# Attention scores in a fused attention and MLP kernel: one 64-row matmul per head, two heads in turn into two PSUM banks

## The chip, the cores and the metric

The kernel runs on one core of a Trainium2 chip. The metric is device time in microseconds (us) of one execution; before the change it is 1000.22 us, the median of three runs.

## The reference

```
k_p = k.reshape(B, H, Sp, 8, D).mean(axis=3)      # B = 8 batches, H = 8 heads, S = 576 tokens, D = 64
v_p = v.reshape(B, H, Sp, 8, D).mean(axis=3)      # Sp = 72 pooled keys
scores = scale * np.matmul(q, k_p.transpose(0, 1, 3, 2))
attn = np.exp(scores - max); attn = attn / (sum + 1e-09)
x = (attn @ v_p), heads side by side              # 4608 tokens x 512
h = x @ w_in                                      # 512 x 2048
out = (h * sigmoid(1.702 * h)) @ w_out            # 2048 x 512
```

All inputs are float32 or, for the weights, float64 on the way in; the output is 4608 x 512 float32.

## The kernel before

Two parts share the core. The first is attention; it writes `x`, transposed, as pairs of float32r values (a high and a low part). The second is the MLP: `moe_in` (L555 to L573) multiplies 128 columns of `w_in` by chunks of 256 or 384 tokens into PSUM tiles `h`, and `moe_out` (L575 to L589) multiplies by `w_out` into PSUM tiles `o`. Each MLP product is three float32r passes (L563 to L565, L583 to L585). The MLP loop at the end of the kernel goes over the steps of all chunks, and after each step it calls `pump()` some five times; a pump runs the attention generator up to its next `yield`. A chunk of the MLP cannot start before its tokens of `x` are written, and attention may not run further ahead than two buffers of `x`. The framework then orders the instructions of each engine with a timeline of its own, so that code order is a priority rather than an order.

Attention goes batch by batch, and each batch in two pieces of tokens: piece 0 has two tiles of 128 tokens, piece 1 two tiles of 128 and one of 64. In the code `j` counts the four pairs of heads. For a pair, `turned_q(j)` makes `qt`, the queries turned to 128 rows (64 columns of head 2j, then 64 of head 2j+1) by tokens; from the second batch on this is a DVE transpose (L296) of a tile `qr` that four DMAs fetch. `sum_keys` and `turn_keys` make `m.k2`, in which each pair has 128 rows by 144 columns on a block diagonal: rows 0 to 63 hold the first head's keys in columns 0 to 71, rows 64 to 127 the second head's in columns 72 to 143, and zeros stand elsewhere. So `score` (L305) needs one matmul per pair and tile of tokens: the stationary operand is `qt` (128 rows by 128 or 64 tokens), the moving one `m.k2[:, j]`, and the 144 columns of the result are both heads' scores. Scores are plain float32 matmuls. `less_most` (L317) then takes each head's maximum on DVE (L320) and subtracts it on the way from PSUM to the SBUF tile `sc` (L321); ACT's exponential (L354), sums and the normalised `main` and `tail` follow (L359, L381, L389).

`qt` and `qr` have two buffers each. The PSUM pool `ps_a` has three banks, which the scores (`sps`), the turned keys (`kps`) and the weighted values (`pav`, L452 to L455) share. Between the pairs the generator yields, so `score(j)`, `turned_q(j + 2)` and `less_most` of pair j take turns with MLP work.

Of the kernel before, what the change touches and what calls it, by code (L numbers as in the profile page):

```python
# [22 lines left out]
def attention_moe_kernel(ctx: ExitStack, tc: tile.TileContext, q, k, v, w_in, w_out, out):  # L23
    """Every float32 product is three float32r passes: an operand x is hi + lo, hi the rounding of
    x to 12 significant bits and lo the exact rest, and hi*hi + hi*lo + lo*hi carries float32's bits."""
# [15 lines left out]
    # Tokens of a batch in two pieces, and each piece's tiles of tokens: first token and count.  # L41
# [6 lines left out]
    OVER = 192  # tokens of a piece beyond its first chunk, at most  # L48
# [7 lines left out]
    # The chunks of tokens of the second part: first token and count.  # L56
# [63 lines left out]
    def fetch_q(b, piece, j, place=None):  # L120
        """Quadrants of 32 partitions: a head of the pair and half of its columns each."""
# [14 lines left out]
    def spread(b, raw, bd, nm):  # L136
        """The window sums of 64 keys of each head, each pair's two heads on a block diagonal."""
# [31 lines left out]
    def fetch_first():  # L169
        """The first batch, where x and the last parts of the weights will lie; q as it is."""  # L170
# [93 lines left out]
    written = [0]  # tokens whose x is complete  # L264
    unstaged = []

    def attention(b, piece, whole_q=None):
        """In stages; each yield says which chunk must be through before the next stage, or how far it is."""
# [36 lines left out]
        def score(j, qt):  # L305
            ps = ps_a.tile([P, 512], F32, tag="a", name=f"sps{n}_{j}")
            for t, (s0, ns) in enumerate(tiles):
                nc.tensor.matmul(  # L308
                    ps[:ns, t * PW : (t + 1) * PW],
                    lhsT=qt[:, s0 - o0 : s0 - o0 + ns],  # L310
                    rhs=m.k2[:, j],
                    start=True,
                    stop=True,
                )
            return ps

        def less_most(hs, views):  # L317
            for (ns, g), pv in zip(groups, views):
                nt, nh = g.stop - g.start, hs.stop - hs.start
# [4 lines left out]
                    in1=nm[:ns, g, hs].unsqueeze(3).broadcast_to([ns, nt, nh, KEYS]),  # L324
# [7 lines left out]
        for j in range(NJ):  # L332
            ps = score(j, qts[j])
            yield -1
            if j + 2 < NJ:
                qts.append(turned_q(j + 2))
                yield -1
            views = [
                ps[:ns, g.start * PW : g.stop * PW].rearrange("p (t h s) -> p t h s", h=2, s=KEYS) for ns, g in groups
            ]  # L340
# [90 lines left out]
        def tail_parts():  # L431
            """hi twice and lo of the last keys of four heads, in three quadrants of 32 partitions."""
# [30 lines left out]
        def unstage():  # L463
            """Tokens of the next chunk wait until there is room for it."""
# [25 lines left out]
    # The weights in parts of 512 columns: 128 columns of w_in and 128 rows of w_out in turn, the  # L490
    # last rows in halves. Until a part is due, its float64s lie where the part GAP places on will.
# [15 lines left out]
    def decode_weights():  # L507
        """float64 to float32, to nearest, and its two parts. Magnitudes are below 2**128, and those
        under 2**-119 come out within 2**-118. In stages that run behind each other."""
        count, state = len(parts), {}  # L510

        def start(i):
# [12 lines left out]
        def narrow(i):  # L525
# [5 lines left out]
            # As integers, so that a carry goes on into the exponent.  # L531
# [23 lines left out]
    def moe_in(t0, n, fs):  # L555
        """h and g of n tokens for some blocks of 128 columns of w_in, 512 values a partition."""
# [14 lines left out]
        # Pool is free once the weights are decoded.  # L571
# [19 lines left out]
    def stream():  # L591
# [9 lines left out]
        # Each piece is scored before the values of the piece in front of it are summed; at the  # L601
        # start, where x is awaited, they take turns.
# [88 lines left out]
```

## Time and profile before

| | |
|---|---|
| runs | 999.85, 1000.22, 1001.75 us; median 1000.22 |
| profiled execution, first to last instruction | 994.9 us; the page gives no other time of its own, and the runs' median is 5.3 us above |
| PE busy | 939.4 us (94%), 4957 matmul records |
| PEld (weight loads) busy | 835.0 us (84%) |
| DVE, ACT, POOL busy | 551.3 us (55%), 411.9 us (41%), 266.7 us (27%) |
| score matmuls, L308 | 320 records in 57.6 us of busy PE |

A float32 matmul leaves two records (two passes, each with a weight load of its own), a float32r matmul one: 160 score matmuls make 320 records. The end of a matmul's record is modelled, and records overlap, so a matmul's share of PE is read from the distance between starts. The profile gives rows as start, duration, engine, line, operation, result<-operands, stationary rows*columns, and the moving shape; a row with "x6" merges six neighbours.

### The profile page before, as it was taken

Reading aid. Unit: us, or ns where it says so; the run is one execution under the profiler, and the core shown is the slowest. Engines: PE = TensorE matmul, PEld = TensorE weight load, DVE = VectorE, ACT = ScalarE, POOL = GpSimd, SP = SyncE. Lnnn points to the kernel's source line nnn. Section 1 sums busy time; section 2 is a strip of 40 time slices with the busy share of each in tenths; the row PEclk is TensorE's granted clock in tenths of the full one; section 3 lists DMA queues with packets and bytes.
Section 4 is the critical chain, followed back from the end, with each engine's and each line's share of the span. In section 5 each row is a group of like instructions: output and inputs, shape, how many; then the busy total and the mean of one; then the engine's idle time right before and its main releaser. Section 6 shows DMA issues by size and latency. Waiting matters only on the chain.

```text
span 994.9 us, 13412 instructions
## 1 busy us (share of the span) xinstructions
PE 939.4 (94%) x4957; PEld 835.0 (84%) x4957; DVE 551.3 (55%) x1094; ACT 411.9 (41%) x837; POOL 266.7 (27%) x240
## 2 busy tenths in 40 slices
PE   5597899989999999999989999999999999999998
PEld 4476698888878999899978989889988999999997
DVE  3999995789989660760788560680685410100000
ACT  3788553444336432452434342442445332322222
POOL 2568620111212222222212222222212322222222
PEclk8689799999999999999999999999999999999999
DMA  8984341312233030130223030130010000000000
GB/s 208 340 241 126 74 102 32 77 35 52 71 54 85 32 70 1 43 75 1 60 42 85 32 69 1 38 70 1 33 27 1 33 1 0 33 1 1 33 1 32
DMA packets 100449, 57.50 MB, mean 58 GB/s; under 512 B 75168, under 2 KB 83360, under 8 KB 100384
## 3 DMA queue, kind: packets, MB, share of 16 engines
q1 hardware_dynamic: 95200, 47.21, 19.6%
q10 hardware_dynamic: 5184, 9.44, 2.6%
q8 instruction: 39, 0.64, 0.3%
q14 instruction: 26, 0.21, 0.1%
HBM read 47.19 MB, written 9.44 MB: 57 GB/s over the span
## 4 chain that ended last, share of the span: by engine, by line
PE 63%; DVE 18%; DMA 6%; issue 4%; ACT 4%; SPq 3%; POOL 1%; DVEq 0%; ACTq 0%; POOLq 0%
PE h L565 10%; PE o L585 10%; PE h L564 10%; PE o L583 10%; PE h L563 10%; PE o L584 10%; DVE main L389 7%; DMA qr<-in_q_dram 2%; PE sps L308 2%; DMA tl<-in_v_dram 1%; DMA raw<-in_moe_w_out_dram 1%; SPq L183 1%; DVE al L426 1%; DVE tail L381 1%; DVE red_k L147 1%
## 5 line engine op out<-in xcount | busy, mean ns | idle before, releaser
L572 POOL TENSOR_TENSOR gl<-g,gh 128x384 fp32r<-128x384 f32 (+1 forms) x168 | 176.0, 1047 | 619.1 <-ACT g L570 595.6
L564 PE MATMUL h<-x,w 128*128 128x384 f32 (+1 forms) x832 | 274.0, 329 | 4.1 <-POOL w L543 3.5
L565 PE MATMUL h<-x,w 128*128 128x384 f32 (+1 forms) x832 | 273.5, 329 | 1.4 <-DVE x L459 1.4
L563 PE MATMUL h<-x,w 128*128 128x384 f32 (+1 forms) x832 | 273.6, 329 | 0.5 <-ACT x L458 0.4
L569 ACT ACTIVATE gh<-h 128x384 fp32r<-128x384 f32 (+1 forms) x184 | 93.0, 505 | 337.6 <-PE h L565 333.8
L583 PE MATMUL o<-w,gh 128*128 128x512 f32 x576 | 227.9, 396 | 2.6 <-ACT gh L569 2.5
L584 PE MATMUL o<-w,gh 128*128 128x512 f32 x576 | 227.8, 395 | 0.0
L585 PE MATMUL o<-w,gl 128*128 128x512 f32 x576 | 192.0, 399 | 3.3 <-DVE gl L572 3.0
L564 PEld LDWEIGHTS h<-x,w 128*128 128x128 f32 x832 | 160.2, 193 | 14.0 <-POOL w L543 4.1
L563 PEld LDWEIGHTS h<-x,w 128*128 128x128 f32 x832 | 159.9, 192 | 10.8 <-issue 0.8
L565 PEld LDWEIGHTS h<-x,w 128*128 128x128 f32 x832 | 159.2, 192 | 8.0 <-DVE x L459 1.6
L426 DVE TENSOR_TENSOR al<-mt,ah 128x256 fp32r<-128x256 f32 (+1 forms) x56 | 31.9, 569 | 180.1 <-PE pav L454 142.6
L583 PEld LDWEIGHTS o<-w,gh 128*128 128x128 f32 x576 | 108.7, 189 | 19.6 <-ACT gh L569 3.8
L585 PEld LDWEIGHTS o<-w,gl 128*128 128x128 f32 x576 | 106.2, 189 | 22.4 <-DVE gl L572 3.6
L584 PEld LDWEIGHTS o<-w,gh 128*128 128x128 f32 x576 | 108.8, 189 | 16.5 <-issue 0.4
L389 DVE TENSOR_TENSOR main<-sc,sm 32x256 f32<-32x256 f32 (+1 forms) x224 | 118.5, 529 | 3.2
L570 ACT ACTIVATE g<-h 128x384 f32<-128x384 f32 (+1 forms) x184 | 92.1, 501 | 13.8 <-DVE gl L572 6.9
L459 DVE TENSOR_TENSOR x<-pav,x 128x256 fp32r<-128x256 f32 (+3 forms) x64 | 24.9, 390 | 68.0 <-ACT x L458 67.9
L308 PE MATMUL sps<-k,qt 128*128 128x144 f32 (+1 forms) x320 | 57.6, 305 | 2.8 <-DVE sc L321 2.7
L308 PEld LDWEIGHTS sps<-k,qt 128*128 128x128 f32 (+1 forms) x320 | 45.4, 187 | 10.9 <-DVE sc L321 2.9
L532 POOL TENSOR_TENSOR raw<-raw 128x512 uint32<-128x512 uint32 (+1 forms) x33 | 41.5, 1261 | 40.8 <-DVE raw L528 14.5
L425 ACT CAST ah<-mt 128x256 fp32r<-128x256 f32 (+1 forms) x56 | 24.3, 434 | 52.9 <-DVE mt L422 39.6
(80 smaller groups left out, 891.7 us busy)
## 6 DMA issues: line engine op xcount, KB each, us to landing
out_dram<-osb ACTq DMA_DIRECT2D x36, 256.0 KB
raw<-in_moe_w_in_dram SPq DMA_DIRECT2D x16, 512.0 KB
raw<-in_moe_w_out_dram SPq DMA_DIRECT2D x15, 512.0 KB
kv_False<-in_k_dram SPq DMA_DIRECT2D x28, 256.0 KB
kv_True<-in_v_dram SPq DMA_DIRECT2D x28, 256.0 KB
qr<-in_q_dram SPq DMA_DIRECT2D x112, 40.0 KB
qr<-in_q_dram SPq DMA_DIRECT2D x112, 32.0 KB
tl<-in_v_dram SPq DMA_DIRECT2D x48, 64.0 KB
```

The source lines that it names most:

```text
L308: nc.tensor.matmul(ps[:ns, t * PW : (t + 1) * PW], lhsT=qt[:, s0 - o0 : s0 - o0 + ns], rhs=m.k2[:, j], start=True, stop=True,)
L389: nc.vector.tensor_tensor(out=main[32 * r : 32 * (r + 1), :, cols].rearrange("p j t k -> p t j k"), in0=sc[rows, 0:nt, a::2, 32 * half : 3 ...
L426: nc.vector.tensor_tensor(out=al[:, :npc], in0=pt[:, :npc], in1=ah[:, :npc].bitcast(F32), op=ALU.subtract)
L563: nc.tensor.matmul(o, lhsT=w[:, 0, j], rhs=x[:, 0, j], start=j == 0, stop=False)
L564: nc.tensor.matmul(o, lhsT=w[:, 1, j], rhs=x[:, 0, j], start=False, stop=False)
L565: nc.tensor.matmul(o, lhsT=w[:, 0, j], rhs=x[:, 1, j], start=False, stop=j == NJ - 1)
L569: nc.scalar.activation(out=gh, in_=h, func=AF.Gelu_apprx_sigmoid)
L570: nc.scalar.activation(out=g, in_=h, func=AF.Gelu_apprx_sigmoid)
L572: (nc.vector if c < 2 else nc.gpsimd).tensor_tensor(out=gl, in0=g, in1=gh.bitcast(F32), op=ALU.subtract)
L583: nc.tensor.matmul(o, lhsT=gh[:, i, tok], rhs=w[:, 0], start=f == 0, stop=False)
L584: nc.tensor.matmul(o, lhsT=gh[:, i, tok], rhs=w[:, 1], start=False, stop=False)
L585: nc.tensor.matmul(o, lhsT=gl[:, i, tok], rhs=w[:, 0], start=False, stop=f == NF - 1)
```

## The change

The scores of one head become one matmul with 64 contracted rows: the head's half of `qt` against its own 72 columns of `m.k2` in the same 64 rows. The zeros of the block diagonal are no longer multiplied. Two pairs of heads (four heads) are scored together, into two PSUM banks: bank 0 takes the first heads of both pairs (rows 0 to 63), bank 1 the second heads (rows 64 to 127), and in the code the two take turns. `less_most` then runs once for each bank, on two heads of the same half. Both pairs' `qt` must be there before `score`, and the next two pairs are turned behind it, one after the other. A piece has two yields fewer. Comments were dropped elsewhere, which moves the line numbers by up to five: `score`'s matmul is L312, `less_most` is L325 and L326.

```
-        def score(j, qt):
-            ps = ps_a.tile([P, 512], F32, tag="a", name=f"sps{n}_{j}")
+        def score(j, pair):
+            banks = [ps_a.tile([P, 512], F32, tag="a", name=f"sps{n}_{j}_{a}") for a in range(2)]
             for t, (s0, ns) in enumerate(tiles):
-                nc.tensor.matmul(
-                    ps[:ns, t * PW : (t + 1) * PW],
-                    lhsT=qt[:, s0 - o0 : s0 - o0 + ns],
-                    rhs=m.k2[:, j],
-                    start=True, stop=True,
-                )
-            return ps
+                for i in range(2):
+                    for a in range(2):
+                        rows, c0 = slice(a * D, (a + 1) * D), (2 * t + i) * KEYS
+                        nc.tensor.matmul(
+                            banks[a][:ns, c0 : c0 + KEYS],
+                            lhsT=pair[i][rows, s0 - o0 : s0 - o0 + ns],
+                            rhs=m.k2[rows, j + i, a * KEYS : (a + 1) * KEYS],
+                            start=True, stop=True,
+                        )
+            return banks
...
-        for j in range(NJ):
-            ps = score(j, qts[j])
+        for j in range(0, NJ, 2):
+            banks = score(j, qts[j : j + 2])
             yield -1
             if j + 2 < NJ:
                 qts.append(turned_q(j + 2))
                 yield -1
...
-            less_most(slice(2 * j, 2 * j + 2), views)
-            yield -1
+                qts.append(turned_q(j + 3))
+                yield -1
+            for a, bank in enumerate(banks):
+                less_most(slice(2 * j + a, 2 * j + a + 3, 2), bank)
+                yield -1
```

PE's order in piece 0 of the seventh batch, before, where the keys have just been turned (`kps`): `sps_0_0` is the PSUM tile of the first pair, `o` and `h` are the MLP's, and x2 stands for the two tiles of tokens.

```order
L563 MATMUL h_3_5689<-x_4598,w_3_265 128x384
L230 MATMUL kps_1_5531<-ident,kbd_5500 128x2x64 x2
L233 MATMUL kps_1_5531<-ident,tbd_5501 128x4x8
L308 MATMUL sps_0_0_5563<-k_5525,qt_0_0_5549 128x144 x2
L585 MATMUL o_5649<-w_1_223,gl_1_5645 128x512
L585 MATMUL o_5653<-w_1_223,gl_1_5645 128x512
L585 MATMUL o_5657<-w_1_223,gl_1_5645 128x512
L564 MATMUL h_3_5689<-x_4598,w_3_265 128x384
```

The same place on PE in the changed kernel: `sps_0_0_0` is bank 0 (the first heads) and `qt_0_0`, `qt_0_1` are the two pairs; the two score rows come again for the second tile of tokens before the MLP goes on.

```order
L568 MATMUL h_3_5817<-x_4698,w_3_275 128x384
L230 MATMUL kps_1_5651<-ident,kbd_5620 128x2x64 x2
L233 MATMUL kps_1_5651<-ident,tbd_5621 128x4x8
L312 MATMUL sps_0_0_0_5683<-k_5645,qt_0_0_5669 128x72
L312 MATMUL sps_0_0_0_5683<-k_5645,qt_0_1_5676 128x72
```

What stood as two full matmuls is now four half ones, all of bank 0 and so all on rows 0 to 63; those of bank 1 (`sps_0_0_1`) come eighteen MLP matmuls later, in a run of their own. The framework's order, not the code's, decides that. The last two pairs of the same piece stand as the code has them, the heads in turn (again followed by the same four rows for the second tile):

```order
L590 MATMUL o_5785<-w_3_288,gl_3_5832 128x512
L312 MATMUL sps_0_2_0_5701<-k_5645,qt_0_2_5693 128x72
L312 MATMUL sps_0_2_1_5702<-k_5645,qt_0_2_5693 128x72
L312 MATMUL sps_0_2_0_5701<-k_5645,qt_0_3_5695 128x72
L312 MATMUL sps_0_2_1_5702<-k_5645,qt_0_3_5695 128x72
```

Here all eight score matmuls stand together, where two runs of two stood before. From the fourth batch on every piece 0 has runs of 4, 4 and 8 score matmuls (bank 0, bank 1, in turn), and from the third on every piece 1 has runs of 6, 6 and 12; before, a piece 0 mostly had four runs of 2 and a piece 1 four runs of 3. In all there are 54 runs of 320 score matmuls, where 60 runs of 160 stood.

DVE's order at the same piece, before: `qt_0_2` is turned ahead of the first pair's maximum `nm_0`, `qt_0_3` ahead of the second's; `mt`, `al`, `vbd` and `red` are other steps of attention.

```order
L296 STREAM_TRANSPOSE qt_0_2_5566<-qr_0_2_5551 128x256
L320 TENSOR_REDUCE nm_0_5547<-sps_0_0_5563 128x2x2
L422 STREAM_TRANSPOSE mt_1_0_6066<-main_1_4936 128x320
L150 TENSOR_TENSOR vbd_6142<-red_v_6146,mask_84 128x256
L321 TENSOR_TENSOR sc_0_5546<-sps_0_0_5563,nm_0_5547 128x2x144
L426 TENSOR_TENSOR al_1_0_6069<-mt_1_0_6066,ah_1_0_6068 128x320
L296 STREAM_TRANSPOSE qt_0_3_5573<-qr_0_3_5558 128x256
L320 TENSOR_REDUCE nm_0_5547<-sps_0_1_5570 128x2x2
```

And in the changed kernel:

```order
L325 TENSOR_REDUCE nm_0_5667<-sps_0_0_0_5683 128x2x2
L427 STREAM_TRANSPOSE mt_1_0_6194<-main_1_5056 128x320
L150 TENSOR_TENSOR vbd_6270<-red_v_6274,mask_84 128x256
L326 TENSOR_TENSOR sc_0_5666<-sps_0_0_0_5683,nm_0_5667 128x2x2x72
L431 TENSOR_TENSOR al_1_0_6197<-mt_1_0_6194,ah_1_0_6196 128x320
L427 STREAM_TRANSPOSE mt_1_1_6207<-main_1_5056 128x320
L147 TENSOR_REDUCE red_k_6929<-kv_0_False 128x128
L296 STREAM_TRANSPOSE qt_0_2_5693<-qr_0_2_5671 128x256
L296 STREAM_TRANSPOSE qt_0_3_5695<-qr_0_3_5678 128x256
L325 TENSOR_REDUCE nm_0_5667<-sps_0_0_1_5684 128x2x2
L326 TENSOR_TENSOR sc_0_5666<-sps_0_0_1_5684,nm_0_5667 128x2x2x72
```

Both transposes now stand behind the whole of bank 0's work and wait for the last matmul of bank 1, which frees both `qt` buffers; bank 1's maximum stands behind them.

On SP's queue the fetches of `qr` move by a few places against those of `tl` and `kv`, and early on two fetches of weights (`raw`) fall behind the second batch's first keys.

More of the change, by code (lines that the diff above doesn't have):

```diff
@@ L303, in attention, with less_most @@
         sm = att.tile([P, NT, H], F32, tag="sm", name=f"sm{n}")
-        def score(j, qt):
-            ps = ps_a.tile([P, 512], F32, tag="a", name=f"sps{n}_{j}")
+        def score(j, pair):
+            banks = [ps_a.tile([P, 512], F32, tag="a", name=f"sps{n}_{j}_{a}") for a in range(2)]
             for t, (s0, ns) in enumerate(tiles):
-                nc.tensor.matmul(
-                    ps[:ns, t * PW : (t + 1) * PW],
-                    lhsT=qt[:, s0 - o0 : s0 - o0 + ns],
-                    rhs=m.k2[:, j],
-                    start=True,
-                    stop=True,
-                )
-            return ps
-        def less_most(hs, views):
-            for (ns, g), pv in zip(groups, views):
-                nt, nh = g.stop - g.start, hs.stop - hs.start
+                for i in range(2):
[5 more added lines that the diff above has]
+                            rhs=m.k2[rows, j + i, a * KEYS : (a + 1) * KEYS],
+                            start=True,
+                            stop=True,
+                        )
+            return banks
+        def less_most(hs, bank):
+            for ns, g in groups:
+                nt = g.stop - g.start
+                pv = bank[:ns, 2 * g.start * KEYS : 2 * g.stop * KEYS].rearrange("p (t h s) -> p t h s", h=2, s=KEYS)
                 nc.vector.tensor_reduce(out=nm[:ns, g, hs], in_=pv, axis=AX.X, op=ALU.max, negate=True)
@@ L323, in less_most @@
                     in0=pv,
[L324 removed]
+                    in1=nm[:ns, g, hs].unsqueeze(3).broadcast_to([ns, nt, 2, KEYS]),
                     op=ALU.add,
@@ L337, in attention @@
                 yield -1
-            views = [
-                ps[:ns, g.start * PW : g.stop * PW].rearrange("p (t h s) -> p t h s", h=2, s=KEYS) for ns, g in groups
-            ]
-            less_most(slice(2 * j, 2 * j + 2), views)
-            yield -1
+                qts.append(turned_q(j + 3))
[3 more added lines that the diff above has]
+                yield -1
         if b == 0:
```

## The prediction

> **What bounds the kernel now.** I read the page first: the head, the slices, the shares of the chain of waits.
>
> ```profile
> span 994.9 us, 13412 instructions
> PE 939.4 (94%) x4957; PEld 835.0 (84%) x4957; DVE 551.3 (55%) x1094; ACT 411.9 (41%) x837; POOL 266.7 (27%) x240
> PEclk8689799999999999999999999999999999999999
> PE 63%; DVE 18%; DMA 6%; issue 4%; ACT 4%; SPq 3%; POOL 1%; DVEq 0%; ACTq 0%; POOLq 0%
> ```
>
> PE carries most of the chain, but not everywhere, so the second view is busy time by stretch, over all instructions and then over the score line L308 alone (PE first, PEld second):
>
> ```profile
> 0.00:150.00 150.00, 112.62 (x609) 94.64 (x609) 132.90 (x216) 96.54 (x177) 82.06 (x65) 0.85 0.65 181
> 150.00:225.00 75.00, 70.77 (x441) 63.45 (x442) 54.80 (x122) 31.49 (x60) 7.74 (x6) 0.98 0.22 48
> 225.00:303.00 78.00, 73.31 (x396) 62.89 (x395) 72.44 (x157) 34.83 (x73) 13.65 (x12) 1.00 0.27 58
> 303.00:756.00 453.00, 448.39 (x2326) 401.51 (x2325) 264.53 (x548) 183.17 (x380) 104.42 (x100) 1.00 0.18 42
> ...
> 0.00:150.00 150.00, 11.68 (x56) 9.21 (x56) 0.85 0.65 181
> 150.00:225.00 75.00, 7.39 (x40) 5.59 (x40) 0.98 0.22 48
> 225.00:303.00 78.00, 9.70 (x56) 7.49 (x56) 1.00 0.27 58
> 303.00:756.00 453.00, 28.83 (x170) 23.11 (x168) 1.00 0.18 42
> ```
>
> A batch is 40 score records. The first 150 us (56 records, 1.4 batches) belong to DVE, busy 132.9 of 150. From 150 to 225 (40 records, one batch) PE is busy 70.8 of 75 and DVE only 54.8. From 225 to 303 (1.4 batches) both are near full. From 303 to 756 (4.2 batches) PE is busy 448.4 of 453 and DVE has 188 us to spare. After 756 there are no scores. So PE's time counts fully in 5.2 batches, by about half in 1.4, and hardly in 1.4.
>
> What a score matmul costs on PE is the distance between starts. The timeline of PE, one run of a piece 0 and one of a piece 1:
>
> ```profile
> 489.99 0.39 PE L584 MATMUL o<-w,gh 128*128 128x512 f32 x1
> 490.22 0.65 PE L308 MATMUL sps<-k,qt 128*128 128x144 f32 x4
> 490.62 0.73 PE L585 MATMUL o<-w,gl 128*128 128x512 f32 x2
> 491.18 0.39 PE L583 MATMUL o<-w,gh 128*128 128x512 f32 x1
> ...
> 302.25 0.39 PE L583 MATMUL o<-w,gh 128*128 128x512 f32 x1
> 302.48 1.04 PE L308 MATMUL sps<-k,qt 128*128 128x144 f32 x6
> 303.45 0.50 PE L584 MATMUL o<-w,gh 128*128 128x512 f32 x1
> 303.79 0.40 PE L585 MATMUL o<-w,gl 128*128 128x512 f32 x1
> ```
>
> A 512-column MLP matmul takes 0.23 (489.99 to 490.22). The four passes of two full tiles take 491.18 - 490.22 - 2 x 0.23 = 0.50, or 0.12 a pass. The six of a piece 1, whose last two have 64 stationary columns, take 0.97, and the MLP matmul behind them 0.34 in place of 0.23: 1.08 in all, 0.36 above 6 x 0.12 = 0.72. That 0.36 is what two changes of the stationary shape cost, from 128 columns to 64 and back.
>
> **The change part by part.** *Weight loads.* A pass has its own load, and the load of the next pass runs under the present one. How long it takes is seen where nothing hides it:
>
> ```profile
> 303.45 0.19 PEld L584 LDWEIGHTS o<-w,gh 128*128 128x128 f32 x1 [0.20 <-issue]
> 303.56 0.19 PEld L585 LDWEIGHTS o<-w,gl 128*128 128x128 f32 x1
> ```
>
> The second load starts 0.11 after the first, just the 0.11 that the MLP matmul lost. So 128 columns of weights occupy the loader for 0.11. Before, 0.12 of streaming covered it. Now a pass streams 72 columns where it streamed 144, by proportion 0.06, and there are twice as many passes, each with its 128 columns of queries to load. Whether 64 rows load faster than 128 is answered by the groups of weight loads by shape:
>
> ```profile
> L230 PEld LDWEIGHTS kps<-ident,kbd 128*128 128x128 f32 x32 | 4.1, 144 | 3.5 <-DVE kbd L150 2.7
> L233 PEld LDWEIGHTS kps<-ident,tbd 32*128 32x128 f32 x16 | 2.2, 136 | 5.8 <-DVE tbd L210 3.1 <-issue 2.3 <-DVE sc L321 0.4
> ```
>
> 32 rows take 136 ns and 128 rows 144: hardly. So I take 0.11 for a pass of a 128-token tile, bound by its load, where two such passes replace one of 0.12; bounds are 0.05 (both halves at work at once, 0.11 for two) and 0.21 (the load not hidden, 0.11, plus the stream 0.06 and an emptying of 0.04, below; in all 64 such passes of a batch that would be 6.4 us more, which I leave out, since equal shapes load ahead in every row above). A pass of a 64-token tile loads 64 columns, half of 0.11, and streams 0.06: 0.06, twice as many, so no loss.
>
> *Shape changes.* Every run of scores now leaves the 128-row shape and returns to it. The nearest row is the 32-row step of the turned keys:
>
> ```profile
> 340.06 0.38 PE L230 MATMUL kps<-ident,kbd 128*128 128x128 f32 x2
> 340.37 0.24 PE L233 MATMUL kps<-ident,tbd 32*128 32x32 f32 x1
> 340.55 0.50 PE L585 MATMUL o<-w,gl 128*128 128x512 f32 x1
> 340.88 0.39 PE L583 MATMUL o<-w,gh 128*128 128x512 f32 x1
> ...
> 340.37 0.13 PEld L233 LDWEIGHTS kps<-ident,tbd 32*128 32x128 f32 x1 [0.17 <-issue]
> ```
>
> The two transposes take 0.31 where two passes need 0.11 each: 0.09 to empty the array. The 32-row load then starts together with its matmul, not under the one before. From there to the next is 0.18: 0.11 load, 0.03 stream (32 of 72 columns at 0.06), 0.04 emptying. The MLP matmul behind takes 0.33, 0.10 too long. A run of n loads by this costs 0.09 + 0.11 n + 0.06 + 0.04 + 0.11 = 0.30 + 0.11 n. Within a piece 1 the change from 128 to 64 columns comes on top, half of the 0.36 above less one emptying and one stream that are counted already: 0.18 - 0.04 - 0.06 = 0.08.
>
> *A batch.* Piece 0 has runs of 8, 8 and 16 passes: 3 x 0.30 + 32 x 0.11 = 4.42, before 4 x 0.50 = 2.00. Piece 1 has two runs with 8 passes of full tiles and 4 of the small one, 0.30 + 0.88 + 0.24 + 0.08 = 1.50 each, and one with 16 and 8, 0.30 + 1.76 + 0.48 + 0.08 = 2.62; together 5.62, before 4 x 1.08 = 4.32. A batch grows by 2.42 + 1.30 = 3.7 us.
>
> By the row of the 32-row step a change of rows empties the array, and it might do so between rows 0 to 63 and 64 to 127 as well, 18 times a batch where the heads take turns: 18 x 0.10 (stream and emptying) = 1.8 us more. But the emptyings in the rows above all stand where the shape changes, and equal shapes follow each other without (the x4 run); both heads have the same shape, 64 rows by 128 columns. So I leave the 1.8 out of the sum and keep it as a rival; no row shows two heads' halves side by side. The Trainium skill, "TensorEngine Tiling (Array Packing)", Key Properties, has it as a rule that changing the tiling mode drains the engine and changing only the tile does not; by it the 18 cost nothing, and the drains of the 32-row step agree.
>
> *DVE.* The maxima and subtractions keep their number and sizes, and their waits go to the side: DVE's two transposes of the next pairs now stand behind bank 0's work and wait for bank 1's last matmul, with bank 1's maximum behind them. The cover is DVE's idle time, 188 us of 453. If that cover is missing, PE waits at the next scores or at `pav`, 1.5 to 2.7 at a time, as PE's waits between 150 and 303 us show:
>
> ```profile
> PE sps L308 <- DVE sc L321: 2.7, 1, 2.7
> PE pav L454 <- DVE al L426: 2.4, 3, 1.3
> PE pav L452 <- DVE sc L321: 1.5, 1, 1.5
> ```
>
> I count nothing for it; its bounds are 0 and 21 us (14 pieces at 1.5), and half of that is a rival. On SP the moved fetches of `qr`, `tl`, `kv` and two weights stay in the stretches that DVE or PE bounds; nothing, with 3 us either way, about the 2.7 above. The other way, longer scores use up some of PE's present waits between 150 and 756, such as those above: -2 us, about a third of their 6.6. Two yields fewer in a piece pace attention sooner, but the chunks it waits for hold it: in PE's order the scores stand at the same MLP matmul as before, within some 30 of 4224. Nothing.
>
> *The sum.* 5.2 x 3.7 = 19.2, half of 1.4 x 3.7 = 2.6, less 2: +19.8 us. The profiled 994.9 becomes 1014.7; the runs' median 1000.22 is 5.3 above the span and becomes 1020.
>
> **The rivals.** *The two heads run at once* where they take turns. For it: the two halves use separate rows and separate banks. Then 16 of 32 passes of piece 0 and 24 of 48 of piece 1 cost half: 8 x 0.11 + 8 x 0.11 + 4 x 0.06 = 2.0 less a batch, +1.7 in place of +3.7, and 5.9 x 1.7 - 2 = +8 (5.9 is 5.2 and half of 1.4): 1008. Against it: 125 of the 266 neighbours within runs are of the same half. The Trainium skill, "TensorE: Matmul & The Clock Gate", Part 3, says that matmuls on distinct row groups run concurrently and that a load may be pulled ahead when the row group differs; by it 1008 would be the time. No run here shows it yet; 25%.
>
> *Every change of head empties the array*: 3.7 + 1.8 = +5.5 a batch, 5.9 x 5.5 - 2 = +30: 1030. For it the row of the 32-row step; 12%.
>
> *DVE hands PSUM back late*: half of the 14 pieces make PE wait 1.5 more, +10 on the sum: 1030. Against it DVE's idle time after 303; 8%.
>
> *Faster.* Half the rows load in half the time, so that a pass is the stream's 0.06, and the heads also run at once where they alternate. Piece 0: with half a load less in each run, 3 x 0.25 + 16 x 0.06 + 8 x 0.06 = 2.2 for 2.0; piece 1: 3 x 0.33 + 24 x 0.06 + 12 x 0.06 = 3.2 for 4.3; a batch gains 0.9, 5.9 x 0.9 = 5: 995. It decides once a full-tile pass comes below about 0.05 on average; against it stand 136 and 144 ns for 32 and 128 rows. 6%.
>
> *It does not reach the end*, because DVE and not PE sets the pace between 225 and 756: 1000. Against it 448.4 of 453. 4%. That the change does less than it says is seen in the order already: half the scores do not take turns, which the sum includes.
>
> **How the numbers follow.** The forecast has 45%, the rest as above. The range goes from the first rival less 4 for the start and the waits, 1004, to the second and third plus 6, 1036; outside it are faster and no effect, and a tail. Faster by over 0.2% is 6%; within 0.2% (2 us, about what a measurement of this kernel tells from no change: the three runs lie within 1.9 us) 3%; slower 91%.
>
> **What would show it.** Right: score records at twice the number, 0.11 apart in runs of one head and in turn alike; the first load of each run starting with its matmul; the MLP matmul behind each run at 0.33; PE busy up by about 20 us, DVE's unchanged. Runs in turn at 0.05 apart would show the first rival, 0.2 the second; new rows of PE waiting for `sc` or `nm` the third. A score stretch after 303 us that is no longer than before would make the prediction wrong.

## The result and the profile after

The changed kernel takes 1048.99 us (median of four runs, 1046.02 to 1053.31), the kernel before 1000.04 us (four runs, 999.47 to 1001.75). The ratio is 1.0496, with a 95% interval of 1.0467 to 1.0524: 49 us slower, beyond the forecast's 1020 and beyond its range, which ended at 1036.

The profiled execution took 1053.31 us, of which 1051.5 is the span; it is the slowest of the four, 4.3 above their median. The profile before, with its span of 994.9, is of an execution some 3 us below its runs' median (a later run of that kernel with this span took 997.04). So sizes read from the two traces add up to 56.6 and not to 49. Three lines of its page answer to those quoted in the prediction:

```profile
span 1051.5 us, 14040 instructions
PE 977.5 (93%) x5277; PEld 865.3 (82%) x5277; DVE 552.0 (52%) x1094; ACT 416.6 (40%) x839; POOL 264.5 (25%) x240
PEclk8568999999998999999999999999998999999999
```

The span grew by 56.6. PE is busy 38.1 longer, so it also idles more, though it bounds the kernel; DVE does the same work (551.3 before); and two slices of PEclk (the 13th and the 31st), which read 9 before, now read 8.

To see where, I cut both programs at the same work: the start up to PE's 400th MLP matmul, the middle from there to just behind the last score, and the end. PE's first matmul comes 7.7 us into the span before and 9.2 after; a length called the start is counted from there, while the views count from the span's first instruction. First the middle of the kernel before, then start and middle of the changed one, in busy time by stretch (from:to, length, then PE, PEld, DVE, ACT, POOL, PEclk, DMA):

```profile
151.60:754.40 602.80, 590.82 (x3151) 526.29 (x3152) 388.69 (x817) 248.70 (x510) 125.71 (x118) 1.00 0.19 45
```

```profile
0.00:161.80 161.80, 121.17 (x665) 100.96 (x666) 135.29 (x209) 98.77 (x178) 81.04 (x65) 0.82 0.61 173
161.80:809.30 647.50, 619.02 (x3410) 549.20 (x3409) 388.17 (x826) 249.23 (x508) 123.58 (x117) 0.97 0.17 41
```

The middle holds 6.6 batches and 44.7 of the 56.6 us. The start is 8.7 longer, PE's first matmul comes 1.5 later, and the end grew by 1.7 (240.5, then 242.2). In the middle PE's idle time (length less busy) went from 12.0 to 28.5, and the mean granted clock from 1.00 to 0.97: between 150 us and the last microseconds there are seven falls to half speed, 37.5 us together, where before had one of 3.4.

Three things are mixed in this, and the distances between starts of PE's matmuls part them. A distance behind a score pass, up to 0.5, is score time. What an MLP or attention matmul's distance has beyond its usual one (0.23 for 512 columns, 0.17 for 384) is waiting where the clock is full and the excess over 0.25; where the granted clock is 0.5, it is half-clock cost. Scores that run at half clock stay score time. The split is good to about 1 us. For the profiled runs of all kernels of this study, in us (the last three columns are of the middle):

| kernel | start | middle | of it scores | waiting | half clock |
|---|---|---|---|---|---|
| before | 143.9 | 602.8 | 38.0 | 14.2 | 1.1 |
| after | 152.6 | 647.5 | 52.8 | 31.3 | 15.0 |
| full matmuls, two pairs together | 151.2 | 606.0 | 38.6 | 14.7 | 3.6 |
| after, q in long runs | 151.9 | 640.8 | 54.3 | 27.2 | 9.4 |
| after, GAP 1, four `qr` | 180.1 | 617.5 | 46.2 | 17.9 | 6.5 |
| after, heads apart | 157.3 | 643.3 | 62.6 | 15.7 | 16.3 |
| after, 2 KB freed (control) | 154.4 | 640.8 | 51.0 | 27.1 | 12.5 |
| control, four `qr` | 152.9 | 629.2 | 54.0 | 10.7 | 12.6 |
| before, 2 KB freed, four `qr` | 153.9 | 602.8 | 37.5 | 12.5 | 3.6 |
| after, 128 rows x 72 columns | 148.0 | 642.8 | 60.6 | 26.1 | 10.5 |
| before, 128 rows x 72 columns | 155.4 | 627.3 | 58.9 | 17.5 | 6.2 |
| 128 rows x 72 columns, four `qr` | 156.5 | 630.6 | 56.4 | 18.7 | 6.9 |

So of the middle's 44.7 us, scores are 14.8, waiting 17.1, the half clock 13.9. The next three views show each.

**Scores.** PE's timeline of the changed kernel, first a run of one head, then one with the heads in turn (both in pieces 0), and one in turn of a piece 1:

```profile
620.55 0.40 PE L588 MATMUL o<-w,gh 128*128 128x512 f32 x1
620.88 1.11 PE L312 MATMUL sps<-k,qt 64*128 64x72 f32 x8
621.92 0.50 PE L589 MATMUL o<-w,gh 128*128 128x512 f32 x1
622.26 0.39 PE L590 MATMUL o<-w,gl 128*128 128x512 f32 x1
...
774.78 0.39 PE L590 MATMUL o<-w,gl 128*128 128x512 f32 x1
775.10 1.12 PE L312 MATMUL sps<-k,qt 64*128 64x72 f32 x16
776.14 0.41 PE L457 MATMUL pav<-ah,vh 128*128 128x320 f32 x1
...
807.38 1.51 PE L312 MATMUL sps<-k,qt 64*128 64x72 f32 x24
808.82 0.45 PE L570 MATMUL h<-x,w 128*128 128x384 f32 x1
```

Eight passes of one head take 1.04, sixteen in turn the same 1.04. A pass of one head costs 0.11, the load; in turn two heads share 0.11. The MLP matmul ahead of a run takes 0.33 (620.55 to 620.88) and the one behind 0.34, each 0.10 or 0.11 over 0.23. The run of eight so costs 1.24 to 1.25, where the prediction's 0.30 + 0.11 n gives 1.18. In piece 1 a run of 24 in turn takes 1.44 (807.38 to 808.82), and the records of the runs of twelve of one head 1.43.

**Waiting.** The longest waits in the middle, of the kernel before and then of the changed one (us in total, times, longest; SPq is the queue of DMA issues):

```profile
PE pav L454 <- DVE al L426: 6.6, 7, 1.5
PE o L583 <- ACT gh L569: 0.7, 2, 0.4
...
DVE qt L296 <- DMA qr<-in_q_dram: 7.7, 4, 3.5
ACT sc L354 <- DVE sc L321: 24.6, 10, 4.0
SPq L130 <- DVE nm L320: 266.2, 20, 55.6
```

```profile
PE pav L459 <- DVE al L431: 10.0, 5, 2.8
PE o L588 <- ACT gh L574: 7.1, 4, 3.1
PE h L568 <- ACT g L575: 3.7, 2, 2.0
...
DVE qt L296 <- DMA qr<-in_q_dram: 15.6, 5, 5.5
ACT sc L359 <- DVE sc L326: 33.9, 10, 7.0
SPq L130 <- DVE qt L296: 229.7, 8, 61.0
```

PE hardly waits for score banks. It waits for the MLP's own `g` and `gh` (10.8, where it was 0.7 before) and for `al`. The SP line says why: the fetch of `qr` (L130) now waits for the transposes `qt` themselves, and there are two `qr` buffers. One such place, from the timeline of the changed kernel, all engines:

```profile
383.70 1.22 PE L312 MATMUL sps<-k,qt 64*128 64x72 f32 x16 [0.46 <-DVE qt L296]
384.35 0.46 DVE L326 TENSOR_TENSOR sc<-sps,nm 128x288 f32<-128x288 f32 x1
384.67 7.39 SPq L130 DMA_DIRECT2D qr<-in_q_dram  x12
389.70 0.51 DVE L296 STREAM_TRANSPOSE qt<-qr 128x320 f32<-128x320 f32 x1 [4.89 <-DMA qr<-in_q_dram]
391.25 0.78 DVE L326 TENSOR_TENSOR sc<-sps,nm 128x288 f32<-128x288 f32 x2
392.07 1.17 ACT L359 ACTIVATE sc<-sc 128x1152 f32<-128x1152 f32 x1 [3.04 <-DVE sc L326]
392.74 0.31 PE L458 MATMUL pav<-ah,vl 128*128 128x320 f32 x1
393.25 1.28 ACT L575 ACT_TABLE_LOAD   x1
394.55 0.49 ACT L575 ACTIVATE g<-h 128x384 f32<-128x384 f32 x1
395.09 0.45 PE L568 MATMUL h<-x,w 128*128 128x384 f32 x1 [2.05 <-ACT g L575]
395.57 0.52 PE L570 MATMUL h<-x,w 128*128 128x384 f32 x1
```

The queries of two pairs are transposed together, so both `qr` buffers come free together and the fetches of the next piece's first pairs are issued in one row from 384.67, behind four fetches of keys. DVE, which works in order, stands 4.89 at the next piece's first transpose with this piece's last subtractions (L326) behind it. ACT's exponential of 1152 values needs them and comes 3.04 late; the gelu `g` stands behind it and a table load of 1.28 in ACT's queue; and PE, which needs `h`'s PSUM tile back, stands 2.05. Two steps of DVE that the prediction called covered reach PE through ACT.

**The half clock.** At 395.5 the granted clock falls, and the last row of that view already shows 0.52 where 0.33 is usual. Six of the seven falls follow a 3.4 us stretch in which PE idled 0.9 to 2.6 us. One does not; the busy time of its stretch and of the next:

```profile
190.70:194.10 3.40, 3.40 (x29) 2.79 (x27) 1.84 (x6) 0.00 (x0) 0.00 (x0) 1.00 0.15 23
194.10:197.50 3.40, 3.40 (x15) 3.14 (x15) 1.56 (x6) 1.08 (x3) 0.00 (x0) 0.50 0.30 48
```

PE is busy the whole 3.40, 2.3 of it with score passes of half the rows, and the clock falls all the same.

### The profile page after: what moved, and what is told of

It reads as the page before. It is cut to its first block, busy times and chain, and to the rows that moved or that the text cites. A ratio compares the mean times of both kernels' runs of the same rounds, so it can differ in the third digit from the quotient of the medians.

```text
span 1051.5 us, 14040 instructions
## 1 busy us (share of the span) xinstructions
PE 977.5 (93%) x5277; PEld 865.3 (82%) x5277; DVE 552.0 (52%) x1094; ACT 416.6 (40%) x839; POOL 264.5 (25%) x240
## 2 busy tenths in 40 slices
DMA packets 100452, 57.55 MB, mean 55 GB/s; under 512 B 75168, under 2 KB 83360, under 8 KB 100384
## 4 chain that ended last, share of the span: by engine, by line
PE 59%; DVE 21%; DMA 8%; ACT 5%; issue 4%; SPq 3%; ACTq 0%; DVEq 0%
PE h L570 9%; PE o L588 9%; PE o L590 9%; PE h L568 9%; PE h L569 9%; PE o L589 9%; DVE main L394 6%; PE sps L312 3%; DMA kv_False<-in_k_dram 3%; DMA qr<-in_q_dram 2%; DVE al L431 1%; DVE tail L386 1%; DVE nm L325 1%; DVE qt L296 1%; DVE red_v L147 1%
## 5 line engine op out<-in xcount | busy, mean ns | idle before, releaser
L588 PE MATMUL o<-w,gh 128*128 128x512 f32 x576 | 230.8, 401 | 8.9 <-ACT gh L574 8.9
L589 PE MATMUL o<-w,gh 128*128 128x512 f32 x576 | 230.2, 400 | 0.0
L588 PEld LDWEIGHTS o<-w,gh 128*128 128x128 f32 x576 | 110.0, 191 | 26.9 <-ACT gh L574 10.5
L589 PEld LDWEIGHTS o<-w,gh 128*128 128x128 f32 x576 | 110.2, 191 | 16.4
L431 DVE TENSOR_TENSOR al<-mt,ah 128x256 fp32r<-128x256 f32 (+1 forms) x56 | 31.3, 558 | 170.1 <-ACT x L463 90.4
L312 PEld LDWEIGHTS sps<-k,qt 64*128 64x128 f32 (+1 forms) x640 | 60.5, 192 | 17.6 <-issue 6.5
L312 PE MATMUL sps<-k,qt 64*128 64x72 f32 (+1 forms) x640 | 70.8, 289 | 2.4 <-DVE qt L296 1.7
L537 POOL TENSOR_TENSOR raw<-raw 128x512 uint32<-128x512 uint32 (+1 forms) x33 | 39.3, 1194 | 38.3 <-DVE raw L533 23.3
```

The costliest lines, as they stand in the source:

```text
L312: nc.tensor.matmul(banks[a][:ns, c0 : c0 + KEYS], lhsT=pair[i][rows, s0 - o0 : s0 - o0 + ns], rhs=m.k2[rows, j + i, a * KEYS : (a + 1) * K ...
L431: nc.vector.tensor_tensor(out=al[:, :npc], in0=pt[:, :npc], in1=ah[:, :npc].bitcast(F32), op=ALU.subtract)
L588: nc.tensor.matmul(o, lhsT=gh[:, i, tok], rhs=w[:, 0], start=f == 0, stop=False)
L589: nc.tensor.matmul(o, lhsT=gh[:, i, tok], rhs=w[:, 1], start=False, stop=False)
```

## The experiments

The theories: **passes** (twice as many passes, bound by loads, are the whole loss, and waits and clock follow), **hand-off** (two pairs in one step tie the `qt` and `qr` buffers, DVE and ACT come late and PE waits), and **clock** (half-row runs and waits lower it). Each run was timed in three rounds beside the kernel before, unless it says otherwise.

### Full matmuls, two pairs together

The changed kernel's order of steps with the old matmuls: one bank a pair, 128 rows x 144 columns.

```
+for j in range(0, NJ, 2):
+    banks = [score(j + i, qts[j + i]) for i in range(2)]   # score as before
     ... turned_q(j + 2), turned_q(j + 3), then less_most for each bank
```

> The kernel before with its full 128-row score matmuls, one bank per pair, but in the new order of steps: two pairs scored, then the next two pairs turned, then two pairs' maxima. Theory A (hand-off: queries' buffers freed in twos, so fetches and maxima come later, PE stalls for ACT and DVE, and the granted clock drops behind the stalls) expects 1015 to 1030 us and half-clock stretches after 303 us. Theory B (the half matmuls themselves cost it: their loads, their shape changes, and a clock that drops because half the array is idle) expects 998 to 1003 us and no half-clock stretch after 303 us.

1007.91 us, ratio 1.0091 [1.0076, 1.0106], between the ranges of the two theories. Waiting in the middle is 14.7, as before, against A; one half-clock stretch of 3.4 us stands at 309 us, against B. The order of steps by itself costs PE no waiting; a reason may be that here each bank needs one pair's `qt` alone, so that each `qr` comes free by itself. Of the 11.6 us by which its profiled span is longer, 8.3 come ahead of the middle (7.3 in the start, 1.0 before PE's first matmul) and 3.2 in it; why the start moves is left open below.

### q fetched in long runs

The changed kernel with `q` fetched in descriptors of 1280 or 1024 bytes in place of 128; the order of `q`'s tokens in the result differs.

```
-in_=q[b, 2 * j + a, o0 : o0 + npc, e * 32 : (e + 1) * 32].rearrange("(c i) d -> i c d", i=32),
+in_=q[b, 2 * j + a, o0 : o0 + npc // 2].rearrange("(i c) (h d) -> i (c h) d", i=32, d=32),
```

> The changed kernel, but each fetch of queries reads runs of 1280 or 1024 bytes instead of 128, so that the same bytes come in a tenth of the pieces; the queries then stand in a wrong order. Theory A expects DVE's 15.6 us of waiting for qr between 225 and 812 us to fall below 3 us, PE's stalls before gelu results to shrink, and 1020 to 1035 us. Theory B expects 1045 to 1052 us.

1044.11 us, ratio 1.0451 [1.0435, 1.0467], just under theory B's range and far above A's. Waiting fell by 4 of the 17, and DVE's wait for `qr` was 18.6 (15.6 in the changed kernel), though the program's DMA packets fell from 100452 to 43108. So the size of the pieces is not what makes the queries late; that they are issued late is what the view above shows.

### Four `qr` buffers, paid for by GAP

```
-    GAP = 2
+    GAP = 1
-... name=f"qr{b}_{piece}_{j}", bufs=2)
+... name=f"qr{b}_{piece}_{j}", bufs=4)
```

> The changed kernel with four buffers for the fetched queries instead of two; the room comes from GAP = 1 instead of 2 (a raw part of the weights lies one place on, not two), which can shift the first 150 us by some us. Theory A expects the fetches to be issued a piece earlier, DVE's wait for qr below 5 us, and 1020 to 1035 us. Theory B expects 1045 to 1052 us.

1046.58 us, ratio 1.0477 [1.0452, 1.0501], inside theory B's range. A miss in its design: GAP, by which memory was found, sets where undecoded weights lie, and the start grew from 152.6 to 180.1. In the middle, which holds 480 score passes here where the changed kernel's holds 528, waiting fell to 17.9 and the half clock to 6.5. That agrees with the hand-off, but the time tells nothing.

### Heads apart

All passes of bank 0 ahead of all of bank 1, so that heads never take turns.

```
-for t, (s0, ns) in enumerate(tiles):
-    for i in range(2):
-        for a in range(2):
+for a in range(2):
+    for t, (s0, ns) in enumerate(tiles):
+        for i in range(2):
```

> The changed kernel, but all matmuls of the first heads stand in the code ahead of those of the second heads, so the framework has no reason to take turns. If the two halves of the array run at once only where heads alternate (a pass every 0.065 us in runs that alternate, 0.13 in runs of one head), a batch's three runs cost 2.3 us more: about 1060 us. If the turn-taking does nothing, 1049 us, and passes of both kinds stand equally far apart.

1053.19 us, ratio 1.0548 [1.0518, 1.0578], 4 above the changed kernel and between the two numbers expected. Scores cost 9.8 more in the middle: the overlap of the heads, where the order has them in turn, is worth that. Waiting fell to 15.7 here, so the total moved little; the order of DVE's steps moved too, and this run does not say which change did it. The longest runs now stand alone (PE's timeline):

```profile
450.63 0.34 PE L569 MATMUL h<-x,w 128*128 128x384 f32 x1
450.90 2.93 PE L312 MATMUL sps<-k,qt 64*128 64x72 f32 x24
453.76 0.69 PE L570 MATMUL h<-x,w 128*128 128x384 f32 x1
```

No wait stands near it, and the next MLP matmul takes 0.69 for 0.33: the granted clock is 0.50 from 453.7. Four of this kernel's falls follow such runs.

### Four `qr` buffers with the same start, and its control

The last two parts of undecoded weights share a place, which frees 2 KB a partition; alone (the control), and with four `qr` buffers.

```
-tag = f"w{i + GAP}" if i + GAP < 2 * NF else f"spare{i}"
+tag = f"w{i + GAP}" if i + GAP < 2 * NF else f"spare{min(i, 2 * NF - 1)}"
-... name=f"qr{b}_{piece}_{j}", bufs=2)      # second kernel only
+... name=f"qr{b}_{piece}_{j}", bufs=4)
```

> Control for the next two: the changed kernel with 2 KB a partition freed, by letting the last two raw half parts of the weights share one place. Both theories expect the changed kernel's time within its scatter of schedules, 1043 to 1053 us.

> The changed kernel with the freed 2 KB used for four buffers of fetched queries instead of two, and without the change of GAP that cost the start of the earlier try. If the queries' buffers are what delays the maxima and makes PE stall (the earlier try's time between MLP matmul 400 and the last score fell from 647 to 617 us, and its start grew by 28), the start stays near 152 us and the whole comes to 1012 to 1025 us. If not, 1043 to 1053 us as in the control.

The control takes 1048.11 us (1.0493 [1.0465, 1.0520]), as the changed kernel does; with four buffers it is 1031.68 (1.0318 [1.0280, 1.0356]), 16.4 less, but not the 1012 to 1025 expected. The waits of the control's middle, then those with four buffers:

```profile
PE pav L459 <- DVE al L431: 10.2, 5, 2.9
DVE qt L296 <- DMA qr<-in_q_dram: 20.4, 7, 5.7
ACT sc L359 <- DVE sc L326: 34.0, 10, 5.1
```

```profile
PE pav L459 <- DVE al L431: 3.3, 4, 1.4
ACT sc L359 <- DVE sc L326: 12.6, 7, 5.8
```

DVE no longer waits for `qr` in the middle, the exponential waits 12.6 for 34.0, and PE's waiting fell by 16.4 (27.1 to 10.7). The middle as a whole is 11.6 shorter, since scores cost 3.0 more in this order and seven more MLP matmuls fall into it; that the time fell by just 16.4 as well is in part chance. So the hand-off is shown to be a cause, of some 12 to 16 of the 49 us. The half clock did not follow (12.5 and 12.6).

### The kernel before with four `qr` buffers

> The kernel before with the same shared place and four buffers of fetched queries. Its DVE waits for qr are 7.7 us, most of them not on PE's path: 994 to 1002 us. If it gained as much as the changed kernel does from the buffers (25 us or more), the buffers would be a matter of both kernels and explain nothing of the difference.

The same two edits on the kernel before: 1005.51 us, ratio 1.0060 [1.0038, 1.0082], 3.5 above the expected range. The middle stays at 602.8; the start is 10 longer. So the buffers mend only what the change broke.

### 128 rows x 72 columns in the changed kernel

Steps, banks and runs of the changed kernel, but each pass over all 128 rows; the block diagonal's zeros are multiplied again.

```
-lhsT=pair[i][rows, s0 - o0 : s0 - o0 + ns],
-rhs=m.k2[rows, j + i, a * KEYS : (a + 1) * KEYS],
+lhsT=pair[i][:, s0 - o0 : s0 - o0 + ns],
+rhs=m.k2[:, j + i, a * KEYS : (a + 1) * KEYS],
```

> The changed kernel's steps, banks, runs and buffers, but each score matmul contracts all 128 rows (72 columns of the block diagonal, zeros included), so that there is no change of rows and no half-used array. Passes should be 0.11 apart in every run, runs of one head and in turn alike. If the clock drops because the gate counts the half-row runs as idle, the half-clock stretches that follow runs of scores without a stall vanish, and only those behind a stall of 2 us stay. If the stalls come from the banks and buffers, they stay: 1030 to 1045 us. If the half-row matmuls are what makes both, 1008 to 1020 us.

1043.22 us, ratio 1.0447 [1.0418, 1.0476], against 1.0496 [1.0467, 1.0524], and inside the range for stalls that come from banks and buffers. Full rows lose the overlap (scores 60.6 for 52.8) and spare the shape change at the ends of runs and part of the half clock (10.5 for 15.0). PE's timeline of a run of 24 passes:

```profile
795.65 0.34 PE L569 MATMUL h<-x,w 128*128 128x384 f32 x1
795.82 2.54 PE L312 MATMUL sps<-k,qt 128*128 128x72 f32 x24
798.29 0.44 PE L570 MATMUL h<-x,w 128*128 128x384 f32 x1
```

The run takes 2.47; the matmul ahead keeps its 0.17, and no fall of the clock follows. So the gain and the price of half rows nearly cancel here, and the bulk of the loss comes without them: with two passes of 72 columns for one of 144, and two pairs in a bank.

### 128 rows x 72 columns in the kernel before

The kernel before, one bank a pair and pair by pair, its matmul cut in two. This parts the count of passes from the banks.

```
+for a in range(2):
     nc.tensor.matmul(
-        ps[:ns, t * PW : (t + 1) * PW],
+        ps[:ns, t * PW + a * KEYS : t * PW + (a + 1) * KEYS],
         lhsT=qt[:, s0 - o0 : s0 - o0 + ns],
-        rhs=m.k2[:, j],
+        rhs=m.k2[:, j, a * KEYS : (a + 1) * KEYS],
```

> The kernel before, with its steps and its one bank for a pair, but each score matmul of 128 rows by 144 columns is two of 128 rows by 72 columns. Theory A (the count of passes, the tied qt buffers and the clock each have a part of their own): only the passes grow, by 0.112 x 8 - 0.50 = 0.40 a run of piece 0 and about 0.42 a run of piece 1, 3.3 a batch, in 5.9 batches 19: 1019, between 1013 and 1026; PE's waits in the middle of the program stay at the 14 of the kernel before, half-clock time within 5 of it. Theory B (twice the passes make PE's work longer, and waits and clock follow from that by themselves, whatever banks and buffers do): as the kernel with full rows, two banks and 72 columns, 1043, between 1036 and 1050, with waits of 25 or more.

1037.40 us, ratio 1.0378 [1.0358, 1.0399]: above theory A's 1013 to 1026, and inside theory B's 1036 to 1050 but without its waits. Busy time of its middle:

```profile
163.10:790.40 627.30, 612.13 (x3392) 552.32 (x3393) 385.12 (x818) 246.72 (x506) 125.17 (x117) 0.99 0.19 43
```

In the middle theory A holds: scores grew by 20.9 (19 expected), waiting by 3.3, the half clock by 5.1. (The middle grew by 24.5 only, since 23 MLP matmuls moved behind the last score, where the end is 4.9 longer.) What it left out is the start, 11.5 longer: scores there grew by some 6.5 and half-clock time by 4 to 6, in a part that I had taken to be DVE's. Twice the passes thus cost 37 by themselves, and theory B's waits do not come with them (17.5, not 25 or more). The two banks of mixed pairs add 6 (1037.40 to 1043.22), with waiting from 17.5 to 26.1.

### 128 rows x 72 columns with four `qr` buffers

The two edits of the control and its fellow on the kernel of full rows and two banks.

> The changed kernel's steps, banks and runs, with 128 rows x 72 columns a matmul (1043 by itself), and four buffers of qr in place of two, in the 2 KB that the last weight part frees. Theory A (waits come from qr's late fetches, the lower clock partly from waits and partly from half rows): the waits fall from 26 to about 11, the half-clock time from 10 to below 4, since both of its sources are gone; 1043 - 15 - 6 = 1022, between 1016 and 1030. Theory B (the clock falls by the load-bound passes themselves): waits fall alike but the half-clock time stays near 10: 1028 or more.

1034.39 us, ratio 1.0337 [1.0303, 1.0371], outside A's 1016 to 1030 and inside B's 1028 or more. Waiting fell by 7.4 (15 expected) and the half clock by 3.6, to 6.9, between A's below 4 and B's 10; the start grew by 8.5, which takes part of it back. Neither theory is borne out as it stands.

### Half-row runs where nothing waits

Extra matmuls in the MLP's tail of the kernel before, where PE has no idle time: runs of four kinds between the MLP's steps. Each of the two kernels was run once. First runs of 2.2 to 3.1 us:

> The kernel before, with extra matmuls between the MLP's steps after the last score; their results are never read, and the whole time is longer by them and says nothing. They come in runs of about 2.9 us each, of four kinds in turn: full rows x 144 columns, 64 rows x 72 columns of one head, 64 rows x 72 columns with the heads in turn, full rows x 72 columns. Theory A (runs of half-row passes count as idle for the granted clock): the clock falls to half for 3.4 us or more behind most runs of the two 64-row kinds, and behind none of the two full-row kinds. Theory B (only stalls of PE lower the clock): no fall behind any kind, since nothing waits there. Theory C (short streams, not short rows, lower it): a fall behind the three 72-column kinds. Passes: 0.112 apart for one head and for full rows x 72, 0.056 in turn, 0.122 for 144 columns.

No fall followed any run, as theory B has it. But a fall covers steps of 3.4 us, and the one-head runs of 2.83 lay across two of them, with at most 2.4 in one; the kernel with the heads apart fell after 2.67 and more in one. So the runs were made longer than any step:

```
tiles = [ps_a.tile([P, 512], F32, tag="a", ...) for a in range(2)]
for r in range((26, 26, 52, 26)[kind]):
    a = r % 2 if kind == 2 else 0
    rows = slice(0, P) if kind == 3 else slice(64 * a, 64 * a + 64)
    nc.tensor.matmul(tiles[a][:, 0:KEYS], lhsT=k2[rows, 0:P] if kind == 1 else ident[rows],
                     rhs=k2[rows, 0:KEYS], start=True, stop=True)
```

> As the probe before, in the MLP's tail of the kernel before, with runs about twice as long (5.4 us or more), so that each fills a whole 3.4 us stretch of the granted clock wherever it begins: 64 rows x 72 columns of one head with an identity as weights, the same with keys as weights, 64 rows x 72 columns with the heads in turn, 128 rows x 72 columns. Results are never read, and the time says nothing. Theory A (passes of one head's half rows count for the clock as mostly idle): the clock falls to half for 3.4 us or more behind every run of the two one-head kinds and behind none of the others. Theory B (only waits lower it, and the falls behind long score runs have another cause): no fall behind any. Theory C (weights of zeros and ones were the reason that the shorter probe showed no fall): falls behind the runs with keys as weights alone.

PE's timeline, one run of each kind (identity of one head; keys of one head; in turn; full rows):

```profile
907.96 7.93 PE L669 MATMUL probe<-k,ident 64*128 64x72 f32 x50
...
992.07 7.25 PE L669 MATMUL probe<-k 64*128 64x72 f32 x52
...
1009.67 6.03 PE L669 MATMUL probe<-k,ident 64*128 64x72 f32 x104
...
1024.07 5.92 PE L669 MATMUL probe<-k,ident 128*128 128x72 f32 x52
```

And the busy time of the 10.1 us from each of these runs' start, all instructions (PE is busy throughout; the clock is the number behind POOL's):

```profile
907.90:918.00 10.10, 10.10 (x58) 9.91 (x58) 0.00 (x0) 0.00 (x0) 0.00 (x0) 0.67 0.00 0
...
992.00:1002.10 10.10, 10.10 (x62) 9.90 (x62) 0.00 (x0) 1.15 (x3) 0.08 (x1) 0.73 0.21 79
1009.60:1019.70 10.10, 10.10 (x126) 9.62 (x126) 0.00 (x0) 0.87 (x2) 0.79 (x2) 1.00 0.01 2
1024.00:1034.10 10.10, 10.10 (x76) 9.69 (x75) 0.00 (x0) 0.87 (x2) 1.16 (x2) 1.00 0.00 0
```

Theory A: the clock fell in or behind all eight one-head runs, with either weights, and behind none of the four in turn and none of the four of full rows. That half-row runs of one head lower the clock while PE never waits is shown. That full rows with short streams count wholly as busy is not: in the full-row kernel with four `qr` buffers a fall at 223.8 us followed 3.4 us with 1.6 us of waiting and 0.9 of full-row passes, less waiting than any fall without scores had (1.88 at least).

## Why the prediction was wrong, point by point

Of the profiled 56.6 us, start and middle together, scores are 18.6 (14.8 and 3.8), waiting 17.9 (17.1 and 0.8) and the half clock 16.6 (13.9 and 2.7); the other 3.5 are small changes, the end (1.7) and PE's later first matmul (1.5).

**The load bound** was right: 0.11 a pass of one head, from a row of the MLP. So were 0.10 for each change of shape and DVE's unchanged busy time; PE's busy time rose by 38.1, not by about 20.

**"0.11 apart in runs of one head and in turn alike"** was wrong. In turn, a pass costs 0.056; the first rival had this mechanism. Its 1.7 a batch was somewhat low: with 0.09 ahead of a run and 0.11 behind it, a piece 0 now costs 3 x 1.24 = 3.7 for 2.0, a piece 1 2 x 1.63 + 1.64 = 4.9 for 4.3, together 2.3 more. With 6.6 batches that is 15, beside 14.8 of score time (which leaves out what lies ahead and behind, and holds three runs at half clock). The forecast's own 3.7 a batch would have been 24. It counted only 5.9 batches, taking half of 1.4 and all of another 1.4 for DVE's time; the whole middle counted, and the start with 3.8 more. That the forecast's 21.8 for scores lies near the 18.6 measured is luck: too dear a pass, too few batches. The sentence of the Trainium skill behind that rival ("TensorE: Matmul & The Clock Gate", Part 3: distinct row groups run concurrently) agrees with 0.056.

**"I count nothing for it"** is the step that failed most. DVE has 188 us to spare, but that is an average, and what moved was the order: two transposes that need two late fetches, with the last subtractions behind them. Four `qr` buffers took away 16.4 us of PE's waiting and DVE's wait for `qr`, so this term is shown. The bound of 21 held it; the rival, a bank handed back late at +10, had DVE's lateness but the wrong path. The prediction looked for new waits for `sc` or `nm`; the wait came through SP's queue, DVE, the exponential and the gelu behind it.

**"On SP the moved fetches ... nothing, with 3 us either way"** failed with it: these fetches are where it begins.

**"-2 us" for waits used up** had the wrong sign: waiting in the middle grew by 17.1.

**The granted clock** has no term in the sum, the second step that failed. The page of before shows it as a row of nines, which invites leaving it out; it is 13.9 us in the middle. Of the seven falls, three follow waits alone, one half-row scores alone, and three 1.2 to 1.9 us of waiting with 0.8 to 1.4 us of half-row scores in the same 3.4 us; for two of these (1.2 and 1.5) the waits by themselves fall short of the 1.9 of the last section. How the 13.9 divides between the two is not settled: with four `qr` buffers the waits went and the half clock stayed at 12.6, with full rows it was 10.5, with both 6.9.

**"Hardly in 1.4"**: the start is 8.7 longer, of which scores are 3.8 and the half clock 2.7. But the start is 148 to 157 in every variant that leaves GAP alone, also in the two with the old full matmuls (151.2 and 153.9), so that half matmuls are not needed for a longer start. What does it wasn't tried.

**The direction** was right for a reason that outlasts these sizes: halving the contracted rows does not shorten a load, and halving the columns leaves the load as the bound. Were all heads in turn, two passes at 0.056 would equal one of 0.11 to 0.12 and only 64-token tiles and run ends would differ. No version here beat the kernel before.

## What to carry to other kernels

When a matmul is cut into smaller ones, price each pass by its weight load where that is longer than the stream (here 0.11 and 0.06), and pack passes on different row groups next to each other in the order that PE really runs, not in the code's. When two steps are joined, follow every buffer that they now free together to the DMA issue that waits for it, and on to whatever stands in order behind the late data. Treat PE's clock as a resource: a couple of microseconds of waiting, or of passes on half the rows, cost half speed for the 3.4 us or more that follow.

## What the runs showed of the hardware that was not expected

Loads of the two row halves start 7 ns apart (775.205 and 775.212 in the records of the run at 775.10), and so do their matmuls; each half by itself goes at 0.11 a pass.

The granted clock changes in steps of 3.4 us: behind the start the falls last 3.4, 6.8 or 10.2. Over all runs, in stretches without scores, the least waiting in a 3.4 us stretch that a fall followed is 1.88 us (`q` in long runs, from 152.6), and the most without a fall is 2.02 (the control, from 316.1): between them lies what decides. The Trainium skill, "TensorE: Matmul & The Clock Gate", Part 1, has the clock fall after at least one idle window of about 3.4 us; the step agrees, and an idle share of little over half was enough here. Passes of 64 rows x 72 columns of one head count partly as idle: alone in a stretch they lowered the clock after 2.2 us at the earliest (the control's fellow with four `qr` buffers, from 195.5), and not yet after 2.5 in other places (heads apart, from 696.0); stretches with 2.8 to 3.4 us of 128 rows x 72 columns, or of two heads in turn, did not in the eight such runs of the longer probe.
